# Batches 4 to 7: queries ahead of keys and values in the order of loads

## The chip, the core and the metric

The kernel runs on one core of a Trainium2 chip. The metric is device time in microseconds (us), the median of several executions of the whole kernel; less is better. Before the change it is 199.65 us, the median of 6 runs (198.85 to 201.48).

## The reference

Two chained computations, for 8 batches. First an attention in two steps for 8 heads of width 64, with 576 queries, keys and values a head and 32 packed queries `p`; then a gated long convolution along the sequence, done with a Fourier transform of length 576.

```python
def sm_attn(qq, kk, vv):                      # softmax attention, scale 1/8
    a = softmax(scale * qq @ kk.T); return a @ vv
p_packed = sm_attn(p, k, v)                   # 32 rows a head
attn     = sm_attn(q, p_packed, p_packed)     # 576 rows a head
x        = attn, heads side by side           # (8, 576, 512)
x1, x2, x3 = split(x @ w_proj)                # 512 columns each
x2_conv  = irfft(rfft(x2, axis=1) * rfft(filter_fft, axis=0))
out      = (x1 * x2_conv * x3) @ w_out        # (8, 576, 512), float32
```

## The kernel before

**Stages.** A batch goes through four stages. `front` (L609) turns keys and queries so that the head width lies on the partitions, makes the first scores `s1`, their exponentials `e1`, the packed result `pv`, then the second scores `s2` and their normalised exponentials `a2`. `turn` (L772) multiplies the packed rows with the projection weights (`qp`, copied to `qm` by ScalarE) and takes the Fourier transform of `a2` along the sequence (`fp`, copied to `ez`, combined to `fa` on GpSimd; `a2tp` is the turned `a2`). `middle` (L839) makes the spectra (`f`, multiplied by the filter into `tt` on VectorE, combined into `gm` on GpSimd) and the gates `x1`, `x3` (ScalarE copies `x1s`, VectorE makes `w`). `back` (L894) does the inverse transform (`x2`, from `gm`), multiplies by `w` into `y`, multiplies by the output weights (`o`), and ScalarE scales `o` into a float32 tile `os` that SyncE stores. In the profile PSUM tiles `x1`, `x2` and `x3` all appear as `x_b`, and `s1`, `s2` as `s_b`. Buffer numbers are left out there; where a batch is meant, it is given here as `s2` of batch 4, and so on.

The stages of four batches run interleaved (L997 to L1005): while `front` works on batch b, `turn` works on b-1, `middle` on b-2 and `back` on b-3.

**Loads.** `load(b)` (L531) issues three loads on GpSimd's queue: `kn` (keys), `vn` (values) and `qn` (queries), each of 512 to 576 KB of float32 that is cast to float16 on the way. Every one has two buffers, so the load of batch b overwrites that of b-2. Batches 2 and 4 are followed by small loads for several batches (`load_small`, L520: the packed queries `pn` and the last 64 queries `qt`).

**Turning by DMA.** `TURNED, TURNED_K, TURNED_A = 4, 6, 9` (L515). For batches 4 to 7 the queries are turned by one transposing DMA on SyncE's queue, from `qn` into `qT` (L544), instead of on TensorE; for batches 6 and 7 the keys too, by four such DMAs into `kT` (L673). `qT` has two buffers. There is one set of four `kT` tiles, which every batch uses.

**Stores.** The `os` tile has five buffers (L944). Batches 0, 2, 4, 6 make four output tiles, batches 1, 3, 5, 7 five (the fifth holds rows of two batches). A tile is stored by one, two or three DMAs on SyncE's queue; the third tile of a batch needs three (L950 to L954). ScalarE can write the next tile only when the stores of the tile five before it have landed.

**The order of everything.** All operations are first recorded (`Recorder`, L161). `plan` (L258) then orders them: eight rounds of a list schedule (`schedule`), with its own durations for each engine and for DMAs, in which the ready operation with the earliest due time goes first; the round with the earliest end is kept, and `emit` (L445 is the call of every recorded operation, so nearly every row of the profile has that line) issues the operations in this order. Each engine, and the DMA issues among its instructions, runs strictly in this order. In the built program DMAs of GpSimd take eight semaphores in turn, those of SyncE and ScalarE eight others; a DMA also waits until the previous one of its semaphore has landed.

Of the kernel before, what the change touches and what calls it, by code (L numbers as in the profile page):

```python
# [451 lines left out]
def kernel(  # L452
# [11 lines left out]
    nc = Recorder(tc)  # L464
# [21 lines left out]
    def sb(shape, dtype, tag, name, bufs=2):  # L486
        return nc.tile(sbuf, shape, dtype, tag, bufs, name)
# [27 lines left out]
    TURNED, TURNED_K, TURNED_A = 4, 6, 9  # L515
# [4 lines left out]
    def load_small(b, n):  # L520

        pn = const.tile([P, n, 2, D], FP16, tag=f"pn{b}", name=f"pn_b{b}")
        qt = const.tile([P, n, H // 2, D], FP16, tag=f"qt{b}", name=f"qt_b{b}")
        nc.gpsimd.dma_start(pn[:], pflat[:, b:b + n, :, :])
        tail = q[b:b + n, :, 512:576, :].rearrange("b (g u) s d -> u s b g d", u=2)
        for u in range(2):
            nc.gpsimd.dma_start(qt[u * 64:(u + 1) * 64, :, :, :], tail[u])
        for x in range(n):
            small[b + x] = pn[:, x, :, :], qt[:, x, :, :]

    def load(b):  # L531
        if b in (0, 1):
            load_small(b, 1)
        kn = sb([KP, H, KI * D], FP16, tag="kn", name=f"kn_b{b}")
        vn = sb([KP, H, KI * D], FP16, tag="vn", name=f"vn_b{b}")
        qn = sb([P, H, 4 * D], FP16, tag="qn", name=f"qn_b{b}")
        nc.gpsimd.dma_start(kn[:], k[b].rearrange("h (p i) d -> p h (i d)", i=KI))
        nc.gpsimd.dma_start(vn[:], v[b].rearrange("h (p i) d -> p h (i d)", i=KI))
        nc.gpsimd.dma_start(qn[:], q[b, :, 0:512, :].rearrange("h (p i) d -> p h (i d)", i=4))
        if b in (2, 4):  # L540
            load_small(b, b)
        qT = sb([P, H, 2, P], FP16, tag="qT", name=f"qT_b{b}")
        if b >= TURNED:
            nc.sync.dma_start_transpose(qT.rearrange("p h i c -> p (h i) c"), qn.rearrange("p h x -> p (h x)"))  # L544
        loaded[b] = (kn, vn, qn, qT)
# [8 lines left out]
    nc.sync.dma_start(filt[4][0:32, :], ftail[0])  # L554
    nc.sync.dma_start(filt[4][32:64, :], ftail[1])
    load(0)
    wsrc = moe_w_proj.rearrange("(g r) c -> r g c", r=P)
    for c in (1, 0, 2):
        nc.gpsimd.dma_start(wp[:, :, ts(c, DM)], wsrc[:, :, ts(c, DM)])
    nc.sync.dma_start(ac[:], d_ac.ap()[:])  # L560
    load(1)
    nc.gpsimd.dma_start(wout[:], moe_w_out.rearrange("(g r) c -> r g c", r=P))

# [421 lines left out]
    h = prologue_filter()  # L985
# [5 lines left out]
    def ahead():  # L991
        yield from first
        load(2)
        yield from middle(0)
# [55 lines left out]
```

## Time and profile before

| | |
|---|---|
| median of 6 runs | 199.65 us |
| profiled execution, device time | 200.68 us |
| its span (first to last instruction) | 198.7 us |
| mean granted TensorE clock | 0.991 |
| bytes moved by DMA | 32.11 MB; 16.52 MB of them GpSimd's loads, 14.00 MB on SyncE's queue |
| a load of keys, values or queries, issue to landing (median) | 14.2, 14.9, 14.1 us |
| a transposing DMA of queries, of keys (median) | 12.2, 6.0 us |
| a store of 256 KB (median) | 2.9 us |

The rows of one batch come round every 16 to 21 us. The four `gm` additions of `middle`, one row on GpSimd for each batch 1 to 6, start at 70.21, 91.66, 112.34, 131.77, 153.39 and 169.95 us, so the stages between them last 21.45, 20.68, 19.43, 21.62 and 16.56 us.

A row of the timeline gives start, duration, engine, operation, written and read tiles, the shape and the count, and in brackets how long the engine was idle before it and whose end released it. A release is put to the semaphore that came last by the profile; where the engine named had long been done, it was another, often a DMA. TensorE's durations overlap, since matmuls are pipelined.

### The profile page before, as it was taken

Reading aid. Unit: us, or ns where it says so; the run is one execution under the profiler, and the core shown is the slowest. Engines: PE = TensorE matmul, PEld = TensorE weight load, DVE = VectorE, ACT = ScalarE, POOL = GpSimd, SP = SyncE. Lnnn points to the kernel's source line nnn. Section 1 sums busy time; section 2 is a strip of 40 time slices with the busy share of each in tenths; the row PEclk is TensorE's granted clock in tenths of the full one; section 3 lists DMA queues with packets and bytes.
Section 4 is the critical chain, followed back from the end, with each engine's and each line's share of the span. In section 5 each row is a group of like instructions: output and inputs, shape, how many; then the busy total and the mean of one; then the engine's idle time right before and its main releaser. Section 6 shows DMA issues by size and latency. Waiting matters only on the chain.

```text
span 198.7 us, 5698 instructions
## 1 busy us (share of the span) xinstructions
PE 183.7 (92%) x2360; PEld 113.1 (57%) x2360; DVE 140.5 (71%) x264; ACT 123.1 (62%) x261; POOL 133.5 (67%) x108
## 2 busy tenths in 40 slices
PE   4879889999999999999999989997999999999990
PEld 2325664776775765755665656553765565664640
DVE  4236948979278699966896689764698697788610
ACT  2238647768898977867775793827657737416140
POOL 7413477976766999769985992699048995962200
PEclk9999999999999999999999999997899999999999
DMA  5999999999999999999999999998003203503235
GB/s 129 250 286 198 204 203 200 198 199 203 191 235 249 197 197 154 178 217 101 196 195 144 188 185 219 171 171 243 3 8 127 80 0 112 141 16 129 86 69 195
DMA packets 49705, 32.11 MB, mean 162 GB/s; under 512 B 21200, under 2 KB 44240, under 8 KB 49680
## 3 DMA queue, kind: packets, MB, share of 16 engines
q0 software_dynamic: 29312, 16.52, 61.8%
q1 hardware_dynamic: 19360, 14.00, 32.7%
q10 hardware_dynamic: 1008, 1.25, 2.2%
q8 instruction: 18, 0.29, 0.6%
q14 instruction: 7, 0.06, 0.1%
HBM read 35.55 MB, written 9.44 MB: 226 GB/s over the span
## 4 chain that ended last, share of the span: by engine, by line
PE 74%; DMA 7%; POOL 6%; ACT 4%; DVE 3%; issue 2%; SPq 1%; POOLq 0%; ACTq 0%
PE x_b L445 29%; PE o_b L445 15%; PE f_b L445 7%; DMA filt<-in_moe_filter_fft_dram 5%; PE fp_b L445 5%; PE s_b L445 4%; PE pv_b L445 3%; PE kTp_b L445 3%; POOL gm_b L445 2%; POOL tt_b L445 2%; PE qp_b L445 2%; PE hp L445 2%; PE a2tp_b L445 2%; ACT qm_b L445 2%; DMA out_dram<-os_b 1%
## 5 line engine op out<-in xcount | busy, mean ns | idle before, releaser
L445 POOL TENSOR_TENSOR gm_b<-tt_b,tt_b 128x512 f16<-128x512 f32 (+1 forms) x28 | 39.2, 1428 | 6.2 <-DVE tt_b L445 5.8
L445 DVE TENSOR_TENSOR tt_b<-f_b,h 128x1024 f32<-128x1024 f32 x32 | 38.8, 1217 | 5.7 <-PE f_b L445 4.9
L445 PE MATMUL x_b<-a2t_b,qm_b 128*128 128x512 f16 (+1 forms) x256 | 41.0, 290 | 0.0
L445 PE MATMUL x_b<-ac,gm_b 128*128 128x288 f16 (+3 forms) x312 | 37.1, 255 | 1.9 <-POOL gm_b L445 0.8
L445 ACT ACTIVATE os_b<-o_b 128x512 f32<-128x512 f32 x36 | 21.3, 599 | 24.1 <-PE o_b L445 20.0
L445 POOL TENSOR_TENSOR tt_b<-tt_b,tt_b 128x1024 f32<-128x1024 f32 x12 | 28.4, 2364 | 8.7 <-DVE tt_b L445 8.7
L445 PE MATMUL o_b<-wout,y_b 128*128 128x512 f16 x128 | 33.3, 379 | 0.0
L445 ACT COPY x1s_b<-x_b 128x512 f32<-128x512 f32 (+1 forms) x40 | 21.6, 547 | 15.3 <-PE x_b L445 10.1
L445 DVE TENSOR_TENSOR w_b<-x1s_b,x_b 128x512 f32<-128x512 f32 (+1 forms) x40 | 24.8, 628 | 8.5 <-ACT x1s_b L445 6.7
L445 ACT CAST qm_b<-qp_b 128x512 f16<-128x512 f32 x48 | 26.1, 595 | 6.7 <-PE qp_b L445 6.5
L445 PEld LDWEIGHTS <-gm_b 128*128 128x128 f16 x312 | 22.6, 99 | 13.0 <-issue 3.1
L445 POOL TENSOR_TENSOR fa_b<-ez_b 128x512 f16<-128x512 f32 x14 | 17.7, 1274 | 11.6 <-ACT ez_b L445 11.6
L445 DVE SCALAR_TENSOR_TENSOR y_b<-w_b,x_b 128x512 f16<-128x512 f32 x32 | 20.5, 680 | 6.6 <-PE x_b L445 6.6
L445 ACT ACTIVATE e_b<-s_b 96x384 f16<-96x384 f32 (+1 forms) x48 | 23.2, 529 | 2.4 <-PE s_b L445 2.1
L445 PE MATMUL f_b<-qm_b,fa_b 128*128 128x512 f16 x80 | 24.4, 379 | 0.0
L445 POOL TENSOR_TENSOR a_b<-e_b,zr_b 128x1152 f16<-128x1152 f16 (+2 forms) x10 | 17.4, 1744 | 6.5 <-ACT qm_b L445 4.7
L445 PEld LDWEIGHTS <-a_b 128*128 128x128 f16 x240 | 16.1, 98 | 9.6 <-POOL a_b L445 1.2
L445 PEld LDWEIGHTS <-qm_b 128*128 128x128 f16 x256 | 16.1, 99 | 9.4 <-issue 0.5
L445 PEld LDWEIGHTS <-y_b 128*128 128x128 f16 x128 | 11.7, 98 | 11.0 <-DVE y_b L445 0.7
L445 DVE TENSOR_REDUCE zs_b<-e_b 128x36 f32<-128x1152 f16 (+2 forms) x10 | 11.0, 1104 | 1.9 <-ACT e_b L445 1.8
L445 ACT COPY ez_b<-fp_b 128x512 f32<-128x512 f32 x16 | 9.3, 590 | 5.0 <-PE fp_b L445 4.6
L445 PEld LDWEIGHTS <-kT 128*128 128x128 f16 x192 | 8.5, 98 | 3.2 <-issue 0.7
(78 smaller groups left out, 273.1 us busy)
## 6 DMA issues: line engine op xcount, KB each, us to landing
out_dram<-os_b SPq DMA_DIRECT2D x22, 256.0 KB, 2.9
kn_b<-in_k_dram POOLq DMA_DIRECT2D x8, 576.0 KB, 14.2
vn_b<-in_v_dram POOLq DMA_DIRECT2D x8, 576.0 KB, 14.9
qn_b<-in_q_dram POOLq DMA_DIRECT2D x8, 512.0 KB, 14.1
out_dram<-os_b SPq DMA_DIRECT2D x16, 128.0 KB, 2.4
wp<-in_moe_w_proj_dram POOLq DMA_DIRECT2D x3, 512.0 KB, 18.8
filt<-in_moe_filter_fft_dram SPq DMA_DIRECT2D x4, 256.0 KB, 6.7
out_dram<-os_b SPq DMA_DIRECT2D x16, 64.0 KB, 1.8
```

The costliest lines, as they stand in the source:

```text
L445: ins = op.call(*op.args, **op.kw).ins
```

## The change

In `load`, queries are loaded first for batches 4 to 7 and last for batches 0 to 3. The three loads themselves are unchanged.

```diff
@@ -534,9 +534,15 @@
         qn = sb([P, H, 4 * D], FP16, tag="qn", name=f"qn_b{b}")
+        def load_q():
+            nc.gpsimd.dma_start(qn[:], q[b, :, 0:512, :].rearrange("h (p i) d -> p h (i d)", i=4))
+
+        if b >= TURNED:
+            load_q()
         nc.gpsimd.dma_start(kn[:], k[b].rearrange("h (p i) d -> p h (i d)", i=KI))
         nc.gpsimd.dma_start(vn[:], v[b].rearrange("h (p i) d -> p h (i d)", i=KI))
-        nc.gpsimd.dma_start(qn[:], q[b, :, 0:512, :].rearrange("h (p i) d -> p h (i d)", i=4))
+        if b < TURNED:
+            load_q()
         if b in (2, 4):
             load_small(b, b)
```

This is the order in which operations are recorded. The order in which they are issued is the planner's, and it works out anew. The two built programs have the same operations (but for one filler matmul at the start) and differ in their order as follows.

GpSimd's queue from batch 4's loads on (a digit is the batch; `a2`, `tt`, `gm`, `fa` are additions and multiplications):

```
before: kn4 pn qt | fa1 fa1 | qn4 vn4 qt | a2_2 tt1 | kn5     | tt1 fa2 gm1(x4) fa2 | qn5 a2_3 vn5 kn6 tt2 vn6
        fa3 fa3 tt2 gm2(x4) | a2_4 qn6 qn7 kn7 tt3 vn7 ...
after:  kn4 pn qt | fa1 fa1 | vn4 qn4 qt | a2_2 tt1 | qn5 kn5 | tt1 fa2 gm1(x4) fa2 |     a2_3 vn5 kn6 tt2 vn6
        fa3 fa3 tt2 gm2(x4) | qn6 qn7 a2_4 kn7 tt3 vn7 ...
```

Before that, only `kn3` moves, behind the second `gm` of batch 0, and two loads of batch 1 change places.

SyncE's queue from the turning of batch 4's queries on (`o1.1` is the store of the first output tile of batch 1; `o2.3abc` the three stores of the third tile of batch 2):

```
before: qT4 o1.1 qT5 o1.2 o1.3abc o1.4 o1.5ab kT6(x4) o2.1 qT6 qT7 o2.2 o2.3a kT7(x4) o2.3bc o2.4 o3.1 ...
after:  qT4 qT5 o1.1 o1.2 o1.3abc o1.4 o1.5ab kT6(x4) qT6 o2.1 qT7 o2.2 o2.3abc kT7(x4) o2.4 o3.1 ...
```

TensorE's order differs in small exchanges up to the turned keys of batch 5, and from the third key tile of batch 5 on it is the same. The largest exchange: the 16 matmuls `s2` of batch 4 stood inside the last output product of batch 1 and now begin 54 matmuls later, behind the first two turned key tiles of batch 5. ScalarE's and VectorE's orders follow it (the exponentials of these scores, their sums `zs`, `zr`). Around `gm` of batch 1, the first tile of `x2` has three matmuls that read the first two parts of `gm` (288 columns each) and three that read the last two (224 columns): the first of those three moves behind the 16 matmuls `qp` of batch 3, the second behind the next tile's 288-column matmuls, a gate's four and six that turn keys. Everything after the `a2` of batch 4 on GpSimd, and after `o2.4` on SyncE, keeps its order.

## The prediction

> **What bounds the kernel now.** First the page's busy times and slices.
>
> ```profile
> PE 183.7 (92%) x2360; PEld 113.1 (57%) x2360; DVE 140.5 (71%) x264; ACT 123.1 (62%) x261; POOL 133.5 (67%) x108
> ...
> PE   4879889999999999999999989997999999999990
> ...
> PEclk9999999999999999999999999997899999999999
> ```
>
> TensorE is busy 92% of the span and in nearly every slice. What can be won is therefore its holes, and there is one where two things meet: slices 27 and 28 (of 4.97 us, so 134 to 144 us) are the only ones with a granted clock below 9 tenths. Next the stretches around the holes: length, busy time of TensorE, its loads, VectorE, ScalarE, GpSimd, then the granted clock.
>
> ```profile
> 73.05:75.70 2.65, 1.83 (x29) 0.84 (x28) 2.58 (x5) 2.38 (x7) 2.65 (x3) 1.00 1.32 189
> 131.00:141.00 10.00, 8.47 (x80) 4.43 (x79) 3.49 (x8) 5.10 (x11) 7.72 (x6) 0.83 0.66 187
> 110.00:118.00 8.00, 7.46 (x110) 4.43 (x106) 5.82 (x11) 6.87 (x17) 7.92 (x6) 1.00 1.31 187
> ```
>
> The stretch from 131 to 141 us loses 1.53 us of idleness and (1 - 0.83) x 10 = 1.70 us of clock, 3.23 us in all. The same point of the batch before, 110 to 118, loses 0.54 us, at full clock. Why the difference? The chain of waits leaves TensorE there:
>
> ```profile
> 124.57 6.02 SPq L445 DMA_TRANSPOSE kT<-kn_b  x4
> 130.64 6.66 SPq L445 DMA_DIRECT2D out_dram<-os_b  x11
> ```
> ```profile
> 131.85 2.82 DMA out_dram<-os_b
> ...
> 135.98 1.23 DVE tt_b L445
> 137.25 3.69 PE x_b L445 x14
> ```
> ```profile
> 133.73 0.60 ACT L445 ACTIVATE os_b<-o_b 128x512 f32<-128x512 f32 x1 [3.53 <-PE f_b L445]
> 134.75 0.60 ACT L445 ACTIVATE os_b<-o_b 128x512 f32<-128x512 f32 x1 [0.42 <-DMA out_dram<-os_b]
> ```
>
> The first fence is SyncE's queue, the second the chain, the third ScalarE. ScalarE stands 3.53 us before it may write an output tile. TensorE's `o` for it ended at 131.1 and is not what was missing: all five `os` buffers were waiting for stores, and three stores (the second and third of batch 2's third tile at 130.64 and 131.26, the fourth tile's at 131.85) stood behind four transposing DMAs of keys. The store of 131.85 landed at 134.67 and released the tile of 134.75; behind it on ScalarE stand `x1s` and `qm`, behind these `w` and `tt` on VectorE, and `tt` frees the PSUM tile for the `x2` of 137.25. TensorE waits 0.69 and 0.43 us for ScalarE (rows at 134.38 and 135.40) and 0.32 us at 137.25. After 141 us TensorE has no hole up to 170 (9.00 of 9.00 us busy, then 20.00 of 20.00), so a microsecond won here stays won.
>
> **SyncE's queue: where the gain is.** It stood like this before the stall:
>
> ```profile
> 99.01 6.99 SPq L445 DMA_TRANSPOSE kT<-kn_b  x4
> 106.09 0.54 SPq L445 DMA_DIRECT2D out_dram<-os_b  x1
> 107.40 15.97 SPq L445 DMA_TRANSPOSE qT_b<-qn_b  x2
> 123.46 1.00 SPq L445 DMA_DIRECT2D out_dram<-os_b  x2
> ```
>
> The changed order puts all three stores of batch 2's third tile ahead of `kT7`, so the 3.53 us wait loses its cause: these stores landed 1.9 and 2.3 us after issue, and sent near 124.5 they are home some 4 us before `o` ends at 131.1. But the tile behind it needs the fourth tile's store, and that still follows `kT7`. The same entries stand ahead of it in both orders, so it comes sooner only by what SyncE is ahead. Batch 6's queries were awaited at 107.40: load at 98.64, landed 8.7 us later. Changed, this load goes out when `gm` ends, at 96.57, and lands at 105.3; `qT6` then starts when `kT6` ends, at 106.0, since the store of 106.09 now follows. With unchanged durations (11.22 for `qT6`, 0.6 for the store, 4.65 for `qT7`) the queue reaches its next store at 122.6 instead of 123.46: 0.8 us ahead. That is the lower bound. The upper: 11.22 us is a transpose beside four loads; the one of batch 4 took 5.45. Changed, `qT5` goes out near 79 instead of 84.87, and seven stores of batch 1 leave from 84 on instead of 91.44 to 94.91, so this traffic is gone when `kT6` and `qT6` run. With half of the 5.8 us difference SyncE is 3.7 us ahead. The fourth store helps until it lands at 132.7, when its `o` is ready: 2.0 us ahead is enough. I take 2, between the bounds.
>
> Sum: idleness falls from 1.53 to the 0.54 of the batch before, and the clock comes back: 1.0 + 1.70 = 2.7 us. At 0.8 us ahead it is 0.8 us of waiting and 0 to 1.70 of clock. I take the clock as whole, since 73.05 to 75.70 idles 0.82 of 2.65 us and keeps 1.00.
>
> The Trainium skill ("TensorE: Matmul & The Clock Gate", Part 1) has the clock halve after at least one idle window of about 3.4 us. Here it halved with TensorE busy 2.72 of the 4 us before 137, so the row goes further than the rule. By the rule alone the clock would not count and the gain would be 1.0 us.
>
> **A store that moves back.** The store of batch 2's first tile, 106.09 before, now follows `qT6`. It took 12.7 us to land behind `kT6`; `qT6` took 16.2 us from issue and landed at 123.6. Landing with it, near 124, the store frees a buffer that ScalarE writes at 127.85: covered by 4 us, price 0; without that cover one for one.
>
> [...]
>
> **Batch 4 and 5 on GpSimd.** Queries of batch 4 now follow values: one load later, some 3.5 us. `qT4` landed 10.4 us after 69.95, at 80.3; changed about 84, and `s2` of batch 4 reads it at 91.56 before, later still changed. Price 0.
>
> Queries of batch 5 move ahead of their keys, from 76.35 to 65.8. One issue, 0.92 us, enters the row that ends in `gm` (70.21 to 75.17). Bounds: 0 to 0.92 us later. I take 0, because TensorE's order follows: before, it waits 0.41 us for the third and 0.41 for the fourth part of `gm`. Changed, parts end at 72.4, 73.6, 74.9 and 76.1; TensorE waits about 0.4 for the second and 0.35 for the third, and the fourth is read after about 1.8 us of other matmuls, at 76.7. If that cover fails it costs 0.9. Behind 76.35 the issue is gone, so `a2` of batch 3 starts at 77.3 as before. Keys of batch 5 land 3.5 us later than 77.2, read at 94.61: covered.
>
> **Batch 6 and 7 on GpSimd, and the late `s2` of batch 4.**
>
> ```profile
> 96.57 2.13 POOL L445 TENSOR_TENSOR a_b<-e_b,zr_b 128x1152 f16<-128x1152 f16 x1
> 98.64 1.82 POOL L445 DMA_DIRECT2D qn_b<-in_q_dram  x2
> 101.35 0.78 POOL L445 DMA_DIRECT2D kn_b<-in_k_dram  x1 [0.88 <-PE kTp_b L445]
> ```
>
> Here `a2` of batch 4 (the first row) goes behind the two loads, so at 98.4 at the earliest. Its scores come later too: 16 matmuls (0.47 us together) that ran at 91.56 now run near 95.5 to 96.5, two exponentials (1.08) end at 97.2, sums and reciprocals (1.35 and 0.38) at 99.0, `a2` (2.13) at 101.1. TensorE's `fp` of batch 4 reads it at 101.93, so 0.8 us of cover remain. The key load waits for TensorE until 101.35 anyway, and the next `tt` on VectorE, pushed about 1 us by the sums, meets 1.15 us of idleness on GpSimd at 105.67. Bounds 0 and 1.0; I take 0.2, since three engines lose slack at once.
>
> The exchanges before 60 us move the same instructions among themselves: 0, within 0.3 either way.
>
> **Sum.** 2.7 - 0.2 = 2.5 us off a span of 198.7, so 196.2; with the 2.0 us around it 198.2 for the profiled execution, which at 200.68 lies 1.03 above the median of 199.65. Off the median: 197.15, rounded to 197.2.
>
> **Rivals.**
> *SyncE is not ahead.* If `qT6` takes its 11 us or more, or its load lands no sooner, the fourth store lands near 134.7 as before, and `tt` and the `x2` of 137.25 stay where they are. Only the first ScalarE wait goes, which is hidden by the second. For it: the lower bound is only 0.8 us. Against it: the lighter traffic. Time 199.2 to 199.8.
> *The slack of 92 to 106 us is used up.* `a2` of batch 4 comes 1 us or more after 101.9, GpSimd's `tt` and `gm` of batch 3 slip with it, and half the gain is lost: 198.2 to 199.
> *Slower: a load that blocks GpSimd.* The load of batch 7's queries overwrites batch 5's, so it waits for `qT5` to land, and `a2` of batch 4 now stands behind that wait. `qT5` landed at 98.9 before; then `a2` would end at 98.9 + 0.9 + 2.1 = 102.0, costing 0.1. Each us later costs one on `a2`, `fp` and `tt`: from a landing at 101.3 the gain of 2.5 is gone, at 103.8 the kernel takes 202.2. Against it: the load of batch 5's queries goes out 10.5 us sooner, so `qT5` should land near 93.
> *It does not do what it says*: batch 4's queries end up later, and those of 6 and 7 preceded their keys already; only batch 5's move ahead. This holds in any case; the rest is the new plan.
>
> **Chances.** Forecast case 0.62 (own range 196.0 to 198.0), SyncE not ahead 0.20, slack used up 0.08, slower 0.10. The range 196.0 to 199.8 leaves out the slower case and some of each tail. A measurement of this kernel tells about 1% (2 us) from no change. Faster by more than that means under 197.65: most of the first case, 0.54. Slower 0.10; the remaining 0.36 within 1%.
>
> **What would show it.** Right: no slice with a granted clock below 9 tenths; ScalarE's output tiles of batch 3 without a wait over 1 us; `gm` of batch 4 to `gm` of batch 5 at 19 us instead of 21.6; `qT6` on SyncE clearly under 11 us. Wrong: an `os` wait near 134 again; a GpSimd idleness before `a2` of batch 4; a longer step from `gm` of batch 2 to that of batch 3 than 20.7 us; a new low-clock slice elsewhere.

## The result, and the profile after

| | before | after |
|---|---|---|
| median, all executions measured side by side | 199.14 us (63) | 197.63 us (28) |
| ratio after to before, 95% interval | | 0.9939 (0.9923 to 0.9955) |
| profiled execution, its span | 200.68, 198.7 us | 197.4, 195.5 us |
| ratio in a second comparison (27 and 8 executions) | | 0.9918 (0.9889 to 0.9947) |

The ratios, and the table of clocks further down, leave out executions more than 1.5% above the fastest of the same kernel, without which the median before is 198.85 us. The changed kernel is faster by 0.6 to 0.8%, 1.2 to 1.6 us. That is less than the 2.5 us forecast, and the profiled executions differ by more, 3.28 us. So the question is not only where the time went, but which of these numbers is the gain.

The page's busy times and slices of the changed kernel:

```profile
PE 180.1 (92%) x2359; PEld 112.6 (58%) x2359; DVE 140.2 (72%) x264; ACT 123.2 (63%) x261; POOL 133.5 (68%) x108
...
PE   3749979999997999999999989999999999999990
...
PEclk9999999999999999999999999999999999999999
```

No slice has a clock under 9 tenths now. The stretch of the stall, with the columns of the prediction (length, TensorE, its loads, VectorE, ScalarE, GpSimd, clock):

```profile
131.00:141.00 10.00, 9.59 (x170) 6.50 (x169) 6.43 (x11) 7.17 (x16) 7.85 (x7) 1.00 0.54 160
```

TensorE idles 0.41 us there instead of 1.53, at full clock instead of 0.83: 1.12 and 1.70 us. Up to there nothing is won: `gm` of batch 4 starts at 131.79, before at 131.77, and the `x2` behind the stall at 135.75 instead of 137.25. First these two rows of the changed kernel, then SyncE's queue and ScalarE's two output tiles:

```profile
131.79 4.97 POOL L445 TENSOR_TENSOR gm_b<-tt_b,tt_b 128x512 f16<-128x512 f32 x4
135.75 0.53 PE L445 MATMUL x_b<-ac,gm_b 128*128 128x288 f16 x3 [0.32 <-DVE tt_b L445]
```
```profile
106.61 10.64 SPq L445 DMA_TRANSPOSE qT_b<-qn_b  x1
117.35 0.54 SPq L445 DMA_DIRECT2D out_dram<-os_b  x1
118.00 2.88 SPq L445 DMA_TRANSPOSE qT_b<-qn_b  x1
120.97 2.99 SPq L445 DMA_DIRECT2D out_dram<-os_b  x4
124.06 6.30 SPq L445 DMA_TRANSPOSE kT<-kn_b  x4
130.46 5.24 SPq L445 DMA_DIRECT2D out_dram<-os_b  x9
```
```profile
131.16 0.60 ACT L445 ACTIVATE os_b<-o_b 128x512 f32<-128x512 f32 x1 [0.93 <-PE o_b L445]
133.25 0.60 ACT L445 ACTIVATE os_b<-o_b 128x512 f32<-128x512 f32 x1 [1.50 <-PE x_b L445]
```

The first tile no longer waits for a buffer but for its product (`o`), the 3.53 us are gone. The second still waits 1.50 us: the profile names `x`, which had ended, but the fourth tile's store, issued at 130.46 (first of the last row), landed at 133.17. It left 1.39 us sooner than before (131.85).

### The profile page after: what moved, and what is told of

Same layout as the page of the kernel before. It is cut to its first block, busy times and chain, and to the rows that moved or that the text cites. A ratio compares the mean times of both kernels' runs of the same rounds, so it can differ in the third digit from the quotient of the medians.

```text
span 195.5 us, 5695 instructions
## 1 busy us (share of the span) xinstructions
PE 180.1 (92%) x2359; PEld 112.6 (58%) x2359; DVE 140.2 (72%) x264; ACT 123.2 (63%) x261; POOL 133.5 (68%) x108
## 4 chain that ended last, share of the span: by engine, by line
PE 78%; DMA 6%; DVE 5%; POOL 4%; ACT 3%; issue 1%; SPq 0%; POOLq 0%; DVEq 0%
PE x_b L445 30%; PE o_b L445 14%; PE f_b L445 8%; PE fp_b L445 5%; DMA filt<-in_moe_filter_fft_dram 5%; PE s_b L445 5%; PE pv_b L445 3%; PE qp_b L445 3%; PE kTp_b L445 3%; PE hp L445 2%; PE a2tp_b L445 2%; DVE tt_b L445 2%; ACT qm_b L445 1%; POOL fa_b L445 1%; POOL tt_b L445 1%; PE fpt_b L445 1%
## 5 line engine op out<-in xcount | busy, mean ns | idle before, releaser
L445 PE MATMUL x_b<-a2t_b,qm_b 128*128 128x512 f16 (+1 forms) x256 | 40.1, 286 | 0.0
L445 PE MATMUL x_b<-ac,gm_b 128*128 128x64 f16 (+3 forms) x312 | 36.0, 252 | 1.1 <-ACT qm_b L445 0.5
L445 PEld LDWEIGHTS <-gm_b 128*128 128x128 f16 x312 | 22.4, 98 | 10.8 <-POOL gm_b L445 1.9
L445 POOL TENSOR_TENSOR fa_b<-ez_b 128x512 f16<-128x512 f32 x14 | 17.6, 1270 | 11.5 <-ACT ez_b L445 10.3
L445 DVE COPY a2t_b<-a2tp_b 128x576 f16<-128x576 f16 x16 | 7.0, 444 | 4.8 <-PE a2tp_b L445 4.8
```

Source lines behind the costliest of these rows:

```text
L445: ins = op.call(*op.args, **op.kw).ins
```

## The experiments

All edit the planned order by hand, in `emit`, so that nothing else is planned anew: `move(order, these, after)` puts operations behind another, `again(order, these, after, times)` repeats matmuls that write the same values. 2321 to 2324 are `kT7`, 1872 and 1873 the second and third store of batch 2's third tile, 1913 the fourth tile's store.

```diff
-        for op in self.plan():
+        for op in edit(self.plan()):
```

I measure the stall by the time from the start of batch 4's `gm` row to the `x2` behind it: 5.48 us in the profile of before, 3.96 after. Each of the two kernels was profiled once more further down, with 4.86 and 3.54 us; differences of half a microsecond between single profiles therefore lie within their scatter.

**The kernel before, once more.** No edit.

> The kernel before, unchanged, so that the granted clock of each of its executions stands beside its time. The profiled execution of before lost 1.70 us of clock at 137 us, and the prediction counted this whole; the kernel after was measured 1.2 us faster in the median, 3.2 us in the profiled span. Theory 'the clock is lost in a part of the executions only': the times fall into groups about 1.7 us apart, and go with the clock: about half of the executions at 0.998 or more and 197.8 to 199, the others at 0.989 to 0.993 and 199 to 201.5. Rival 'always lost': every execution is near 0.991, and the difference between the profile and the median has another cause.

Measured: 199.32 us, ratio 1.0014 (0.9991 to 1.0038). Its profile has a stall of 4.86 us without the slow clock. The first line is from the kernel before as first profiled, the second from this run:

```profile
137.10:140.50 3.40, 3.25 (x12) 1.59 (x12) 0.54 (x3) 2.51 (x6) 1.70 (x1) 0.50 0.39 98
```
```profile
137.10:140.50 3.40, 3.40 (x45) 2.64 (x44) 1.79 (x5) 3.33 (x9) 2.08 (x1) 1.00 0.32 77
```

Half clock for 3.40 us in one execution, behind a stall of 5.48 us, and full clock in the other, behind 4.86: the 1.70 us are paid in a part of the executions. Time does go with the mean clock. Over the executions of both kernels whose clock was listed (median, and their number):

| mean granted clock | before | after |
|---|---|---|
| 0.993 or more | 199.06 us (45) | 197.41 us (26) |
| 0.986 to 0.992 | 199.83 us (34) | 198.54 us (10) |

The groups lie 0.77 and 1.13 us apart rather than 1.7, and the changed kernel has a lower one too. So there is another place where clock is lost. The rows say more: at an equal clock the changed kernel is 1.65 and 1.29 us faster, as much as over all executions (1.59 in the first row within the second comparison alone, 14 and 5 executions). Half clock for 3.40 us would alone take 0.009 off the mean clock of a span of 198.7 us, so no execution of the first row can hold such a stretch. The gain is there without any change of the clock.

**A filler in the stall.** A filler is a matmul done again that changes no result.

```diff
+    again(order, (2298, 2299), 2299, 2)
```

> The matmul pair of batch 5's first spectrum tile f, which ends at 133.6 us and whose reader on VectorE comes at 135.98, is done three times instead of once: 0.85 us of full-size matmuls in a stretch where TensorE stands 1.44 us. Every wait stays. If the clock is lost because TensorE does too little between 131.7 and 137.5 us, and in a part of the executions: no execution pays there, the median falls by 0.6 to 1.0 us (half of 1.7) and the slower group is gone; the stall itself (ScalarE's 3.53 us before the output tile, x2 at 137.25) stays within 0.2 us. Rival 'the clock has nothing to do with it, or is never lost in the median execution': median as before within 0.2 us, or 0.2 us slower.

Measured: 199.89 us, ratio 1.0033 (1.0007 to 1.0058). The stall kept its length (5.11 us), and 8 of 12 executions still had a clock of 0.986 to 0.990. My expectation fell: most of the executions with a lower clock don't lose it at the stall, and filling it gains nothing in the median.

**The store order alone, and the change without it.**

```diff
+    move(order, (2321, 2322, 2323, 2324), 1873)    # before: kT7 behind the third tile's stores
+    move(order, (1872, 1873), 2324)                # after: two of these stores back behind kT7
```

> The kernel before, only kT7's four transposes moved on SyncE's queue behind the second and third store of batch 2's third tile, as in the changed kernel, with no earlier query load. Theory 'the gain is SyncE's lead, and the fourth tile's store decides': ScalarE's 3.53 us wait before the first tile falls to about 0.9, but the fourth tile's store still leaves near 131.9 and lands near 134.7, the second tile is written at 134.7, x2 starts near 137.2: median 199.1, same as before within 0.4 us. Rival 'the store order is the gain': x2 near 135.8, median 197.6 to 198.0.

> The changed kernel with the second and third store of batch 2's third tile put back behind kT7. Theory 'SyncE's lead decides': kT7 ends some 1 us sooner (near 129.4), the two stores leave at 129.4 to 130.4, the fourth tile's store at 130.5 as in the changed kernel and lands at 133.2; ScalarE writes the two tiles at about 132.6 and 133.25, x2 at 135.75: 197.6, same as the changed kernel within 0.4 us. Rival 'the store order is the gain': x2 back at 137, 198.8 to 199.2.

Measured: 200.06 us, ratio 1.0034 (0.999 to 1.0078), for the first; 198.17 us, ratio 0.9949 (0.9921 to 0.9978), for the second. SyncE and ScalarE of the first, then SyncE and ScalarE of the second:

```profile
125.88 5.87 SPq L445 DMA_TRANSPOSE kT<-kn_b  x4
131.85 4.59 SPq L445 DMA_DIRECT2D out_dram<-os_b  x8
```
```profile
131.50 0.60 ACT L445 ACTIVATE os_b<-o_b 128x512 f32<-128x512 f32 x1 [0.93 <-PE o_b L445]
134.63 0.60 ACT L445 ACTIVATE os_b<-o_b 128x512 f32<-128x512 f32 x1 [2.54 <-DMA out_dram<-os_b]
```
```profile
122.43 6.11 SPq L445 DMA_TRANSPOSE kT<-kn_b  x4
128.60 7.37 SPq L445 DMA_DIRECT2D out_dram<-os_b  x11
```
```profile
132.66 0.60 ACT L445 ACTIVATE os_b<-o_b 128x512 f32<-128x512 f32 x1 [2.14 <-DMA out_dram<-os_b]
133.57 0.60 ACT L445 ACTIVATE os_b<-o_b 128x512 f32<-128x512 f32 x1 [0.32 <-DMA out_dram<-os_b]
```

With the stores first, the first tile's wait is gone as in the changed kernel, and nothing is won: the second tile waits until 134.63, the stall is 5.00 us. With the stores put back, the first tile waits 2.14 us again, and the stall is 3.94 us, as in the changed kernel; the median is 0.5 us over the changed kernel's, but the ratios (0.9949 and 0.9939) can't be told apart. The larger of two waits in a row was not the one that counted. What counts is when the fourth tile's store leaves.

**That store ahead of `kT7`, in the kernel after and in the kernel before.**

```diff
+    move(order, (2321, 2322, 2323, 2324), 1913)
```

> The changed kernel with kT7's four transposes moved behind the fourth tile's store too. Theory 'the fourth tile's store decides': in the changed kernel it left at 130.46 and landed at 133.17, and ScalarE stood 1.50 us for it after an output product that ended at 132.7. Now the store leaves near 124.1, the buffer is free long before, ScalarE writes at 132.7, and x2 starts 0.5 us sooner than in the changed kernel (at 135.2 by its clock): 197.1 us, ratio to before 0.991 instead of 0.994. kT7 ends 0.6 us later (131.0), the scores of batch 7 that read it come at 137.2: covered. Rival 'another wait is already as late' (VectorE's tt on the spectrum tile, the matmuls of qp): x2 stays within 0.15 us of the changed kernel's and the median at 197.6.

> The kernel before, its loads as they were, with kT7's transposes behind all of batch 2's stores. Theory 'the only thing that counts at 131 to 137 us is when the fourth tile's store leaves': it leaves near 126 instead of 131.85, ScalarE writes both tiles as soon as their products end (131.2 and 132.7), x2 starts near 135.3 instead of 137.0 to 137.25, and the median is as good as the changed kernel's or better, 197.2 to 197.9, without any change of a load. Rival 'the earlier query loads bring something of their own': 198.5 or more, x2 after 136.

Measured: after with it 197.87 us, ratio 0.9915 (0.9883 to 0.9948), stall 3.44 us; before with it 197.40 us, ratio 0.9893 (0.9863 to 0.9922), stall 3.43 us. ScalarE in the second:

```profile
131.79 0.60 ACT L445 ACTIVATE os_b<-o_b 128x512 f32<-128x512 f32 x1 [0.93 <-PE o_b L445]
133.37 0.60 ACT L445 ACTIVATE os_b<-o_b 128x512 f32<-128x512 f32 x1 [0.98 <-PE o_b L445]
```

Both tiles wait only for their products, and the stall gives up 0.5 us more than in the first profile of the changed kernel, as expected; the median of the first, 197.1 expected, did not follow. The loads of the second are those of the kernel before: the stall's gain needs no change of them.

**The two parts of the change that can have put SyncE ahead, each alone in the kernel before.** 1592 and 1951 are the loads of batch 6's and 7's queries, 1759 the store of batch 2's first tile; 1226 is batch 5's query load, 1393 the first store of batch 1.

```diff
+    move(order, (1592, 1951), 1485)     # first kernel: loads ahead of a2 of batch 4,
+    move(order, (1759,), 1593)          #   the store behind qT6
+    move(order, (1226,), 983)           # second kernel: batch 5's queries ahead of its keys,
+    move(order, (1393,), 1227)          #   the first store behind qT5
```

> One of the two parts that can have put SyncE ahead, alone: in the kernel before, the loads of batch 6's and 7's queries go ahead of a2 of batch 4 on GpSimd, and the store of batch 2's first tile goes behind qT6 on SyncE; batch 5's order stays. Theory 'the lead is the earlier start of qT6' (the prediction's lower bound of 0.8 us): qT6 starts at 106.1 to 106.4 instead of 107.4 to 108.5, keeps its 10.3 to 11.2 us, the fourth tile's store leaves at 130.9 to 131.2 instead of 131.85, x2 comes 4.3 to 4.6 us after the gm row's start (4.9 to 5.5 before, 3.96 in the changed kernel): median 199.0 to 199.3, half of the gain or less. Rival 'this part is the whole': the store leaves near 130.5, x2 4.0 us after gm, 198.0 or less.

> The other part alone: in the kernel before, batch 5's query load goes ahead of its key load on GpSimd, and qT5 ahead of the first store of batch 1 on SyncE. Theory 'lighter traffic': the stores of batch 1 leave some 6 us sooner, kT6, qT6 and qT7 run beside less; qT6 starts as before (its load goes out behind a2 of batch 4, at 98.6), but qT6 and qT7 take 1 to 3 us less together, and the fourth tile's store leaves at 130 to 131: x2 4.0 to 4.6 us after gm, median 198.3 to 199.0. Rival 'no lead from traffic': qT6 and qT7 as long as before within 0.5 us, the store at 131.85, 199.6.

Measured: the first 199.40 us, ratio 0.9982 (0.9946 to 1.0018); the second 201.45 us, ratio 1.0102 (1.0066 to 1.0137), slower. GpSimd of the first:

```profile
96.65 0.92 POOL L445 DMA_DIRECT2D qn_b<-in_q_dram  x1
99.99 0.88 POOL L445 DMA_DIRECT2D qn_b<-in_q_dram  x1 [2.42 <-DVE y_b L445]
100.89 2.14 POOL L445 TENSOR_TENSOR a_b<-e_b,zr_b 128x1152 f16<-128x1152 f16 x1
```

The load of batch 7's queries waits 2.42 us. VectorE's `y`, which the profile names, is not read by it; `qT5`, whose input it overwrites, landed at 99.43. `a2` of batch 4 behind it starts 4 us later than in the kernel before (100.89 against 96.94 in its second profile), and from `gm` of batch 2 to `gm` of batch 3 it takes 21.75 us instead of 20.69. The stall shrinks to 4.06 us against 4.86 in the second profile of before, and the 0.8 us won there had been lost at `gm` (1.06). SyncE was not ahead: it reached the store behind `qT7` at 123.37 (123.46 and 123.13 in the two profiles of before).

TensorE at `gm` of batch 1, in the second kernel and in the changed one:

```profile
74.47 0.42 PE L445 MATMUL x_b<-ac,gm_b 128*128 128x288 f16 x2 [0.27 <-POOL gm_b L445]
75.70 0.27 PE L445 MATMUL x_b<-ac,gm_b 128*128 128x224 f16 x1 [0.81 <-POOL gm_b L445]
...
76.93 0.64 PE L445 MATMUL x_b<-ac,gm_b 128*128 128x224 f16 x4 [0.41 <-POOL gm_b L445]
```
```profile
73.94 0.53 PE L445 MATMUL x_b<-ac,gm_b 128*128 128x288 f16 x3
74.42 1.07 PE L445 MATMUL qp_b<-wp,ppk 64*32 64x512 f16 x16
75.42 0.64 PE L445 MATMUL x_b<-ac,gm_b 128*128 128x224 f16 x4
```

In both, the load ahead of `gm` makes it later: from the start of batch 2's `a2` to `gm` of batch 1 it is 8.78 us before, 9.68 in the second kernel, 9.98 in the changed one. With TensorE's old order this costs its 0.9 us; the changed kernel reads the parts later, waits for none, and has it back at the next `gm` (20.62 us on instead of 21.45). Nor did SyncE gain: `qT6` took 10.43 us and `qT7` 4.15, and the stall stayed at 5.25 us. Neither theory nor rival had the second kernel slower; of its 2.0 us, 0.9 are these, and the other 1.1 are not traced (9 of its 12 executions had a clock under 0.992).

**Fillers elsewhere.** The eight matmuls of batch 0's second score tile three more times, ahead of TensorE's wait at 24 us; in the second kernel also four matmuls in the waits at 60.6 to 62 us, and the fourth store ahead.

```diff
+    again(order, tuple(range(257, 265)), 264, 3)
+    again(order, (980, 981, 962, 963), 936)
+    move(order, (2321, 2322, 2323, 2324), 1913)
```

> The changed kernel; the eight matmuls of batch 0's second score tile, after which TensorE stands 1.1 us for a2 on GpSimd (until 25.37), are done four times instead of once: 24 small matmuls, 0.65 us, inside that wait. The filler at 133 us left 8 of 12 executions at a clock of 0.986 to 0.990, so most of the executions that lose clock lose it elsewhere. Theory 'they lose it at 22 to 28 us, in kernel before and after alike, depending on how the clock's windows fall': with this filler nearly no execution is under 0.992, median 197.1 to 197.4, 0.4 to 0.8 us under that of the changed kernel. Rival 'they lose it at the other thin place of the changed kernel, 59 to 62 us, or at the start': the share under 0.992 stays between a quarter and a half and the median within 0.3 us of the changed kernel's.

> The two edits before together, and four repeated matmuls (0.85 us) in the two waits at 60.6 to 62 us, where TensorE stands 1.06 us around batch 2's qp. Theory: all thin places are filled, every execution has a clock of 0.993 or more, the spread shrinks to 1 us, median 196.6 to 197.0: the best of all versions, ratio to before 0.988 to 0.990. Rival 'fillers cost as much as they save': 197.4 or more.

Measured: 198.43 us, ratio 0.9938 (0.9905 to 0.9972), 8 of 12 executions under 0.992; and 198.27 us, ratio 0.9913 (0.9879 to 0.9947), three executions at 197.05 to 197.18 with a clock of 0.996 or more and four at 198.27 to 198.50 with 0.983 or 0.984. Both theories fell: filling these places leaves most of the lower clocks, and the second kernel is no faster than the same kernel without fillers (197.87 us, 0.9915). The profile of the first shows another: a clock of 0.52 from 12 to 15.5 us, after TensorE had been busy 0.86 us of the 3 us before that.

**The moved store and the changed kernel on one chip.** No new edit.

> The kernel before with kT7's transposes behind all of batch 2's stores, a second time and beside the changed kernel on one chip. Theory 'the moved store beats the changed load order': 197.3 to 197.8, 0.3 us or more under the changed kernel. Rival 'the six executions of the first time were lucky': within 0.2 us of the changed kernel or over it.

> The changed kernel, unchanged, beside the two parts and the moved store: 197.6 to 198.3, ratio to before 0.992 to 0.996; a part of its executions at a clock under 0.992, where TensorE stood for loads at 9 to 12 us and the clock was halved behind it.

Measured: 198.12 us, ratio 0.9922 (0.9887 to 0.9958), and 197.85 us, ratio 0.9918 (0.9889 to 0.9947). The lead of the moved store was not repeated. Its stall was 3.42 us again, but the changed kernel's, in this second profile, is 3.54:

```profile
132.62 4.96 POOL L445 TENSOR_TENSOR gm_b<-tt_b,tt_b 128x512 f16<-128x512 f32 x4
136.16 0.53 PE L445 MATMUL x_b<-ac,gm_b 128*128 128x288 f16 x3 [0.32 <-DVE tt_b L445]
```

Here `gm` came 0.83 us later than in the first profile, behind a low clock at the start, and the fourth tile's store left no later (130.16 against 130.46). So the moved store is worth 0.5 us against one profile and 0.1 against the other. No version beat the changed kernel beyond doubt.

## Why the prediction was right, and where not

**The place, right.** Nearly all of the profile's difference lies at 131 to 141 us: from `gm` of batch 4 to that of batch 5 it takes 18.53 us (19 forecast) instead of 21.62. In the second profiles, where the stall has full clock in both kernels, it is 18.11 instead of 19.43.

**The wait: 1.0 forecast, and about right.** By TensorE's idleness in the stretch it is 1.12 us against the first profile of before and 0.49 against the second (9.10 of 10.00 us busy); by the stall it is 0.90 and 1.32 for the two profiles of the changed kernel against the second of before. SyncE reached its next store 2.49 us earlier (120.97), within 0.8 to 3.7 and near the 2 taken; in the second profiles 1.05 (122.08 against 123.13). Of the 2.49 only 1.39 were left at the fourth store: the second and third store of the third tile, with the gaps behind them, took 2.04 us (122.02 to 124.06) instead of 1.21 (130.64 to 131.85), and `kT7` 0.28 more. So in this profile 0.5 of the wait stayed, which the moved store then took. The sign "without a wait over 1 us" failed: 1.50, and 1.08 in the second profile.

**Its reason, half wrong.** I gave the larger part of the lead to lighter traffic and a shorter `qT6`. It took 10.64 us against 11.22, far from the 8.3 that half the difference would have given, so the sign "clearly under 11" failed. In six profiles with the changed loads it took 10.2 to 10.8, in the eight others 10.3 to 11.6. What came sooner was the start (106.61 against 107.40) and `qT7` (2.88 against 4.65 us, in the second profile after 3.48); why `qT7` was shorter is not settled. Neither part of the change alone gave a lead of this size. Nor is its usual size known: counted back from `gm` of batch 4, SyncE reached this store 10.82 and 10.54 us ahead in the two profiles of the changed kernel and 8.31 and 9.01 in those of before, and 8.8 to 10.8 in four edited versions of the changed kernel in which nothing ahead of it on the queue was moved.

**The clock: 1.70 forecast as whole, and here the step failed.** It came back in the profile, but in the kernel before it is paid in a part of the executions only. Worse, it was counted twice. The profiled execution, 1.03 us above its median, had lost this clock (the second profile, at 198.79 us, had not); I took the 1.70 off it and then took the 1.03 off as well. The sum gave 198.2 for the profiled execution, which came out at 197.4, below it; the median, 197.2 by the same sum, came out at 197.63. Without the clock the sum would have been 0.8 us, with it 2.5; measured are 1.2 to 1.6. So the rule of the Trainium skill ("TensorE: Matmul & The Clock Gate", Part 1) that was weighed there, with its gain of 1.0 us before the 0.2 are taken off, was nearer to the median than the row of one profile. The halving itself goes against that rule, since TensorE was busy 2.06 of the 3.41 us ahead of it. What the sum without the clock lacks is not clock either: executions of 0.993 or more differ by 1.65 us. The stall accounts for 0.9 to 1.3 us of the gain; where the remainder lies no run shows.

**The number, partly luck.** 197.2 lies close to 197.63 because two errors met: too much clock was taken off, and off a median before of 199.65 us, from six executions, where the many measured beside the changed kernel give 198.85. The same 2.5 us off 198.85 would have given 196.35.

**The prices of nothing, right.** Batch 5's query load: `gm` of batch 1 came 1.21 us later (71.42), over the bound of 0.92, but TensorE's waits of 0.41 and 0.41 us for its parts are gone, and `gm` of batch 3 came on time; where the order did not follow, it cost the 0.9 named for a failed cover. The store behind `qT6` landed at 120.66, needed at 127.88. `a2` of batch 4 in the changed kernel:

```profile
96.94 1.80 POOL L445 DMA_DIRECT2D qn_b<-in_q_dram  x2
99.02 2.12 POOL L445 TENSOR_TENSOR a_b<-e_b,zr_b 128x1152 f16<-128x1152 f16 x1 [0.27 <-ACT e_b L445]
```

It ended at 101.14 (101.1 forecast), `fp` read it at 101.95, and `gm` of batch 3 started at 112.37 against 112.34: the 0.2 us were not paid.

**The rivals.** "SyncE is not ahead" fell at 120.97, and would have been right without batch 5's part: there the store left at 131.59 and `x2` came at 137.00. "The load that blocks GpSimd" did not come true only because `qT5` landed at 87.80 us (93 forecast); with batch 5's queries left where they were, it landed at 99.43, and the wait appeared. So neither half of the change gains alone. That both together need TensorE's new order is argued from the second kernel there; they were not run under the old one. "It does not do what it says" holds, and goes further than I wrote: batch 6's keys are issued ahead of its queries in both orders (`kn6` at 80.46, `qn6` at 98.64 before), so of batches 4 to 7 only batch 5's queries moved ahead of their keys.

## What to carry to other kernels

Of several waits in a row on one engine, the last to end counts, not the longest: ask for each what the next one would then wait for. A loss that stands in one profiled execution, such as a slow clock, may be missing from the median execution; where the profile lies above the median, look whether that difference is the loss itself before taking off both. Here a store on which nothing but a buffer depended was cheap to send early, and the transposes queued ahead of it were what made it dear.

## What the hardware showed that was not expected

The clock was halved in some executions and not in others behind much the same idleness. Two profiles of the changed kernel, first the one shown above, then the second:

```profile
9.30:12.00 2.70, 0.00 (x0) 0.00 (x0) 0.01 (x1) 0.62 (x1) 0.00 (x0) 1.00 1.17 316
12.00:15.50 3.50, 3.19 (x12) 0.97 (x12) 2.05 (x3) 1.24 (x2) 0.74 (x1) 1.00 1.21 264
```
```profile
9.30:12.00 2.70, 0.29 (x3) 0.05 (x1) 0.07 (x1) 0.62 (x1) 0.00 (x0) 1.00 1.16 318
12.00:15.50 3.50, 3.50 (x11) 1.05 (x11) 2.00 (x3) 1.24 (x2) 0.75 (x1) 0.69 1.22 267
```

The one with no matmul at all in these 2.70 us kept its clock at 12 to 15.5 us, the one with 0.29 us of them had 0.69. Five of the twelve later profiles show a low clock at 10 to 17 us and none at the stall.

The clock in the traces explains the pair. It changes only at steps of 3.41 us: in the kernel before it was full for 126.29 us, 37 such steps, and then half for one; in the five later profiles it was half for one step too. Where the steps begin differs from execution to execution. In the first of the two above the idle time falls into two steps, in which TensorE is busy 2.10 us (from 7.18) and 1.82 us (from 10.59). In the second it falls into one, with 1.38 us (9.92 to 13.33), and the half clock is the step behind it (13.33 to 16.74). In all five the step ahead of the half clock has 1.26 to 1.38 us of busy TensorE, and in the nine other profiles no step at 7 to 18 us has less than 1.44. So at this place a step about 40% busy was the border, and the place of the steps decided.

At the stall that number does not hold: the kernel before lost its clock behind a step with 2.06 us of busy TensorE (133.66 to 137.07), and the first edit of the store order kept it behind one with 2.36 (133.68 to 137.10). Of the 28 matmuls in the former, 24 were `qp`, which use 64 x 32 of the array; that such matmuls count for less is a guess that no run tests.

The Trainium skill ("TensorE: Matmul & The Clock Gate", Part 1) says that activity is judged in a free-running window of about 3.4 us, and that a kernel's cold stretch therefore varies from run to run. The steps above agree, with 3.41 us and another beginning in each execution.
